# A written engine order, wide one-hot tables and another division of the q work in linear attention with a hash-routed MoE

## Chip, cores and metric

The kernel runs on one core of one Trainium2 chip. The metric is device time in microseconds of one execution, with every input in device memory (HBM) at the start and the output there at the end. Five engines work side by side, each through its own instructions in their order: TensorE (PE, matrix products; the loading of weights is shown apart as PEld), VectorE (DVE), ScalarE (ACT), GpSimd (POOL) and SyncE (SP). They wait for each other with semaphores. Transfers are started by SP (a hardware queue) or by POOL (a software queue, also for gathers and scatters of rows) and run on sixteen DMA engines.

## The reference

Linear attention over 8 batches and 8 heads, 576 tokens, 64 dimensions, is followed by a mixture of eight experts in which a hash of the token's id picks the expert.

```python
q_s = np.exp(q - np.max(q, axis=-1, keepdims=True))
q_s = q_s / (np.sum(q_s, axis=-1, keepdims=True) + 1e-09)
k_s = np.exp(k - np.max(k, axis=2, keepdims=True))
k_s = k_s / (np.sum(k_s, axis=2, keepdims=True) + 1e-09)
kv = np.einsum('bhsd,bhse->bhde', k_s, v)
x = np.einsum('bhsd,bhde->bhse', q_s, kv)
x = x.transpose(0, 2, 1, 3).reshape(4608, 512)

expert_idx = token_ids * np.int64(2654435761) % np.int64(8)
for e in range(8):
    mask = expert_idx == e
    h = np.maximum(x[mask] @ w1[e], 0.0)        # 512 -> 1024
    out[mask] = h @ w2[e]                       # 1024 -> 512
```

## The kernel before

**Slots.** Each expert has 640 slots: a cell of 72 for each of the 8 batches, and 64 overflow slots for tokens beyond a cell. 640 slots are five blocks of 128 rows. If some cell or overflow overfills, a general path (`_any_routing`) runs instead; it is not taken with these inputs.

**Index** (`_Index`). Tokens lie 36 to a partition on 128 partitions. VectorE takes the expert from the id (L82, L84), builds a one-hot table EH over 8 experts × 36 columns (L88), and from counts and prefix sums (the scan in L147 and `_pick`, L156 and L158) each token's rank and slot. `tables` then turns slots into row numbers: for each of the 36 columns VectorE compares a row of 0..127 with the slot's low seven bits (L252, one 128 × 128 table of zeros and ones for each column), and TensorE adds up 36 products of such a table with BV, the slot's block number times the token's own number (L256). The result is `gidx`, one row number for each slot. A second set of 36 tables (L278, L281) gives `oidx`, the rows of overflowing tokens.

**Keys** (`_Attention.keys`). For each batch SP loads k and v (1.18 MB each, through six raw buffers), ACT takes exp of k (L344), POOL (b < 4) or VectorE (b ≥ 4) casts v to f16 (L347), TensorE adds up 72 products (L354), and VectorE divides by the sums (L357 to L363) into `kvr`, one 128 × 128 block-diagonal matrix for each batch and pair of heads.

**Queries.** POOL gathers rows of q in the order of the slots, five blocks for one expert (L371). `soften` takes exp on ACT (L382) and divides by the sum on VectorE (L384 to L387). `turned` transposes a block on TensorE (four products, L396) and copies it out on VectorE (L398) to qT. `product` multiplies qT with kvr for three batches and two experts at once (L408), and ACT copies the result out (L410) to XT, the input of a pair of experts. `overflow` and `shared` (L418, L421, L431, L437, L439) do this for all overflow slots through tables Q (L684).

**Experts** (`_Moe.expert`). A group of eight products (L472, 128 × 320) gives two of the eight 128-wide slices of the hidden layer for one half of the slots; relu goes to ACT (L477) and VectorE (L479) in turn. After eight groups, five blocks of eight products (L484, 128 × 512) give the output, which VectorE (L488) and ACT (L490) take out in turn, and POOL scatters (L492). POOL also fetches weights, four halves of 0.5 MB for each expert (L453), one expert ahead, in two buffers.

**What sets the order.** The program is written in order of need, and a scheduler places instructions of each engine by its own estimate of readiness. Tiles carry the waits. Ten blocks (experts 0 and 1) and four overflow blocks are prepared ahead of the experts. From then on, while a pair of experts runs, the q work of the next pair waits in `queue`; after each of an expert's 13 steps `side` takes two items out:

```python
            def side():
                for _ in range(2):
                    if queue:
                        queue.pop(0)()
```

Of the kernel before, what the change touches and what calls it, by code (L numbers as in the profile page):

```python
# [40 lines left out]
class _Index:  # L41

    def __init__(self, nc, token_ids, cpool, ipool, ps):
        self.nc, self.ipool, self.ps = nc, ipool, ps
        self.count = 0  # L50
        V = nc.vector
        ids = ipool.tile([128, NCH, 2], I32)
        nc.sync.dma_start(ids[:].rearrange("q m w -> q (m w)"), token_ids.bitcast(I32))

        rowi = cpool.tile([128, CAP], F16)
        self.rowi = rowi
        nc.gpsimd.iota(rowi[:], [[1, CAP]], channel_multiplier=0, allow_small_or_imprecise_dtypes=True)
        pidf = cpool.tile([128, 1], F32)
        self.pidf = pidf
        nc.gpsimd.iota(pidf[:], [[0, 1]], channel_multiplier=1, allow_small_or_imprecise_dtypes=True)  # L60
        eio = ipool.tile([128, E_MOE, NCH], F16)
        nc.gpsimd.iota(eio[:], [[1, E_MOE], [0, NCH]], channel_multiplier=0, allow_small_or_imprecise_dtypes=True)
        bio = ipool.tile([128, NBP, C9], F32)
        self.bio = bio
        nc.gpsimd.iota(bio[:], [[2 * CELL, NBP], [0, C9]], channel_multiplier=0, allow_small_or_imprecise_dtypes=True)

        half = cpool.tile([128, 1], F32)
        V.tensor_scalar(out=half[:], in0=pidf[:], scalar1=63.5, scalar2=None, op0=ALU.is_gt)
        self.half = half

        hrow = ipool.tile([128, 128], F16)
        V.tensor_single_scalar(hrow[:], rowi[:, 0:128], 63.5, ALU.is_gt)
        own = ipool.tile([128, 128], F16)
        V.tensor_scalar(out=own[:], in0=hrow[:], scalar1=half[:, 0:1], scalar2=None, op0=ALU.is_equal)
        lower = ipool.tile([128, 128], F16)
        V.scalar_tensor_tensor(out=lower[:], in0=rowi[:, 0:128], scalar=pidf[:, 0:1], in1=own[:],
                               op0=ALU.is_gt, op1=ALU.mult)
        ones = ipool.tile([128, 128], F16)
        nc.gpsimd.memset(ones[:], 1.0)

        ei = ipool.tile([128, NCH], I32)
        V.tensor_single_scalar(ei[:], ids[:, :, 0], 7, ALU.bitwise_and)  # L82
        ef = ipool.tile([128, NCH], F16)
        V.tensor_copy(ef[:], ei[:])  # L84
        self.ef = ef
        EH = ipool.tile([128, E_MOE, NBP, C9], F16)
        EHf = EH[:].rearrange("p e n c -> p (e n c)")
        V.tensor_tensor(out=EH[:].rearrange("p e n c -> p e (n c)"), in0=eio[:],  # L88
                        in1=ef[:].unsqueeze(1).to_broadcast([128, E_MOE, NCH]), op=ALU.is_equal)
        EC = ipool.tile([128, E_MOE, NBP], F16)  # L90
        with nc.allow_low_precision("counts up to 9"):
            V.reduce_sum(EC[:], EH[:], axis=AX.X)

        pa = ps.tile([128, 2, 512], F32, tag="S")
        NE = E_MOE * NCH
        nc.tensor.matmul(pa[:, 0, 0:NE], lhsT=lower[:], rhs=EHf, start=True, stop=True)
        nc.tensor.matmul(pa[:, 1, 0:NE], lhsT=own[:], rhs=EHf, start=True, stop=True)
        pb = ps.tile([128, 2, 512], F32, tag="S")
        NEN = E_MOE * NBP
        for j in range(2):  # L100
            s = slice(64 * j, 64 * j + 64)
            nc.tensor.matmul(pb[:, j, 0:NEN], lhsT=ones[s, :], rhs=EC[s].rearrange("p e n -> p (e n)"),
                             start=True, stop=True)

        ov_be = ipool.tile([128, B_, E_MOE], F32)
        V.tensor_scalar(out=ov_be[:].rearrange("p (n j) e -> p j e n", j=2),
                        in0=pb[:, :, 0:NEN].rearrange("p j (e n) -> p j e n", n=NBP), scalar1=float(CELL),
                        scalar2=0.0, op0=ALU.subtract, op1=ALU.max)
        ov_eb = ipool.tile([128, E_MOE, B_], F32)
        V.tensor_copy(ov_eb[:], ov_be[:].rearrange("p b e -> p e b"))  # L110
        pb_ = ipool.tile([128, B_, E_MOE], F32)
        self._excl(pb_[:], ov_be[:], B_, E_MOE)
        pe_ = ipool.tile([128, E_MOE, B_], F32)
        self._excl(pe_[:], ov_eb[:], E_MOE, B_)
        self.ov_be, self.ov_eb = ov_be, ov_eb
        run = ipool.tile([128, E_MOE * NBP, C9], F32)
        tot = ipool.tile([128, E_MOE * NBP, C9], F32)
        V.tensor_copy(tot[:], pa[:, 1, 0:NE].rearrange("p (g c) -> p g c", c=C9))
        self._excl(run[:], tot[:], E_MOE * NBP, C9)
        V.tensor_tensor(out=run[:], in0=run[:], in1=pa[:, 0, 0:NE].rearrange("p (g c) -> p g c", c=C9), op=ALU.add)  # L120
        EH4 = EH[:]
        self.rank = self._pick(EH4, run[:].rearrange("p (e n) c -> p e n c", e=E_MOE))

        def mine(t):
            d = self._new(ipool, [128, E_MOE, NBP])
            V.tensor_tensor(out=d[:], in0=t[:, :, :, 1], in1=t[:, :, :, 0], op=ALU.subtract)
            V.scalar_tensor_tensor(out=d[:], in0=d[:], scalar=half[:, 0:1], in1=t[:, :, :, 0],
                                   op0=ALU.mult, op1=ALU.add)
            return d[:].unsqueeze(3).to_broadcast([128, E_MOE, NBP, C9])

        ob = self._pick(EH4, mine(pb_[:].rearrange("p (n j) e -> p e n j", j=2)))
        is_ov = ipool.tile([128, NCH], F32)
        self.is_ov = is_ov
        V.tensor_single_scalar(self.is_ov[:], self.rank[:], float(CELL) - 0.5, ALU.is_gt)
        self.ob = ob
        self.rb = self._pick(EH4, mine(pe_[:].rearrange("p e (n j) -> p e n j", j=2)))

    def _new(self, pool, shape):
        self.count += 1
        t = pool.tile(shape, F32, name=f"ix{self.count}")  # L140
        return t

    def _excl(self, out, x, g, n):

        V = self.nc.vector
        xf = x.rearrange("p g n -> p (g n)")
        V.tensor_tensor_scan(out=out.rearrange("p g n -> p (g n)"), data0=xf, data1=xf, initial=0.0, op0=ALU.add,  # L147
                             op1=ALU.bypass)
        V.tensor_tensor(out=out, in0=out, in1=x, op=ALU.subtract)
        b = self._new(self.ipool, [128, g])  # L150
        V.tensor_copy(b[:], out[:, :, 0])
        V.tensor_tensor(out=out, in0=out, in1=b[:].unsqueeze(2).to_broadcast([128, g, n]), op=ALU.subtract)
# [67 lines left out]
    def tables(self, gidx, oidx, tpool):  # L220
# [53 lines left out]
        for n in range(NBP):  # L274
# [5 lines left out]
            for c in range(C9):  # L280
# [14 lines left out]
                        op1=ALU.min)  # L295
        return ov


class _Raw:


# [495 lines left out]
```

The softmax here doesn't subtract the row's maximum and nothing guards it: scores larger than these inputs give would overflow.

## Time and profile before

| | us |
|---|---|
| median of 14 runs | 284.67 |
| range of these runs | 283.87 to 289.28 |
| the profiled execution's own time | 285.23 |
| its span, from the first to the last instruction | 283.4 |
| first product of an expert (L472) | 117.90 |
| the four pairs of experts end at | 161.56, 201.21, 240.56, 276.5 |

Busy shares over the span: PE 72%, PEld 45%, DVE 63%, ACT 33%, POOL 46%. The mean clock granted to TensorE was 0.836 of full speed.

Lines of a group read: source line, engine, operation, tile written <- tiles read, shapes, count | busy us in total, mean ns of one | idle time of the engine just ahead of them, and what ended it. A table by stretches reads: from:to in us, length, then busy us (and number of instructions) for PE, PEld, DVE, ACT and POOL, the granted clock, the DMA engines' share and GB/s. The line PEclk has one digit for each fortieth of the span: 9 is full speed, 5 is half.

### The profile page before, as it was taken

To read this page: it belongs to the slowest core of one execution; us is meant where nothing else is said; L and a number is where in the kernel's file an instruction comes from. 1 tells how busy PE (TensorE), PEld (TensorE's weight loads), DVE (VectorE), ACT (ScalarE), POOL (GpSimd) and SP (SyncE) were. 2 spreads that over 40 slices of the span, in tenths; PEclk is the share of its full clock that TensorE was granted. 3 is DMA by queue.
4 is the path that set the end of the run, shared out by engine and by line. 5 is a ranking of instruction groups with operands and counts; after the bars stand their busy time and mean duration, and the time that the engine had idled before them with its cause. 6 is when DMAs were issued, how large, how long until landed. Compare 5 with 4: busy or idle time off the path is not lost. (4 is left out here: it accounts for less than half of the span.)

```text
span 283.4 us, 4832 instructions
## 1 busy us (share of the span) xinstructions
PE 202.7 (72%) x1836; PEld 128.9 (45%) x1836; DVE 179.4 (63%) x484; ACT 94.2 (33%) x151; POOL 131.0 (46%) x148
## 2 busy tenths in 40 slices
PE   0070295711313386999969999999999999899990
PEld 0060164601201274574636575665674664655640
DVE  6999995808279994899799269983353231333310
ACT  2532001109215335442842144851222731211210
POOL 9873307435708874218782723614504415315033
PEclk9996555555555556899999999999999999999996
DMA  6999999982623445199988996895969759934022
GB/s 251 425 429 323 317 324 421 418 319 75 167 63 103 129 107 157 12 202 256 237 237 175 205 226 106 214 165 94 239 133 161 206 100 204 193 82 161 0 75 105
DMA packets 13804, 55.38 MB, mean 195 GB/s; under 512 B 2898, under 2 KB 2898, under 8 KB 11728
## 3 DMA queue, kind: packets, MB, share of 16 engines
q0 software_dynamic: 11328, 36.11, 54.5%
q1 hardware_dynamic: 2448, 18.91, 16.3%
q8 instruction: 16, 0.26, 0.4%
q14 instruction: 12, 0.10, 0.1%
HBM read 64.00 MB, written 10.49 MB: 263 GB/s over the span
## 5 line engine op out<-in xcount | busy, mean ns | idle before, releaser
L484 PE MATMUL po<-w2r,hT 128*128 128x512 f16 x320 | 73.3, 379 | 0.0
L371 POOL DMA_INDIRECT qraw<-in_q_dram,gidx x40 | 46.6, 1164 | 41.4 <-ACT q L382 22.4
L492 POOL DMA_INDIRECT out_dram<-ob,gidx x40 | 41.4, 1036 | 50.6 <-DVE ob L488 35.3
L472 PEld LDWEIGHTS <-w1r 128*128 128x128 f16 x512 | 48.8, 98 | 21.0 <-issue 2.7
L472 PE MATMUL ph<-XTn,w1r 128*128 128x320 f16 x384 | 56.9, 299 | 0.9 <-DVE hT L479 0.8
L484 PEld LDWEIGHTS <-hT 128*128 128x128 f16 x320 | 30.6, 98 | 32.7
L488 DVE TENSOR_SCALAR ob<-po 128x512 f32<-128x512 f32 x24 | 16.6, 691 | 44.8 <-PE po L484 22.7
L479 DVE TENSOR_SCALAR hT<-ph 128x640 f16<-128x640 f32 x32 | 26.3, 822 | 21.6 <-PE ph L472 20.0
L396 PE MATMUL pq<-ident,q 128*128 128x128 f16 (+1 forms) x176 | 18.8, 238 | 27.7 <-DVE q L387 15.8
L477 ACT ACTIVATE hT<-ph 128x640 f16<-128x640 f32 x32 | 22.5, 702 | 46.5 <-PE ph L472 44.4
L382 ACT ACTIVATE q<-qraw 128x512 f16<-128x512 f32 x44 | 24.4, 620 | 38.0 <-DMA qraw<-in_q_dram,oidx 13.7
L384 DVE TENSOR_REDUCE rq<-q 128x8 f32<-128x512 f16 x44 | 29.6, 678 | 8.2 <-ACT q L382 8.2
L387 DVE TENSOR_TENSOR q<-q,rq 128x512 f16<-128x512 f16 x44 | 30.0, 685 | 0.1
L344 ACT ACTIVATE k<-t 128x2304 f16<-128x2304 f32 x8 | 16.9, 2117 | 37.7 <-remote 20.3
L396 PEld LDWEIGHTS <-q 128*128 128x128 f16 (+1 forms) x176 | 12.7, 106 | 36.0 <-issue 17.5
L453 POOL DMA_DIRECT2D w1r<-in_moe_w_dram x16 | 9.2, 581 | 40.0 <-PE ph L472 19.5
L354 PE MATMUL pt<-t,k 64*64 64x65 f16 x576 | 20.4, 242 | 6.6 <-DVE rq L385 1.9
L490 ACT ACTIVATE ob<-po 128x512 f32<-128x512 f32 x16 | 9.5, 597 | 46.5 <-PE po L484 39.4
L354 PEld LDWEIGHTS <-k 64*64 64x64 f16 x576 | 17.8, 153 | 7.6 <-issue 5.3
L472 PE MATMUL ph<-XTp,w1r 128*128 128x320 f16 x128 | 19.7, 299 | 0.8 <-ACT hT L477 0.8
L408 PE MATMUL px<-qT,kvr 128*128 128x144 f16 x128 | 14.6, 240 | 5.2 <-issue 2.6
L410 ACT CAST XTn<-px 128x432 f16<-128x432 f32 (+1 forms) x36 | 15.8, 482 | 6.1 <-PE px L408 4.6
(128 smaller groups left out, 186.9 us busy)
## 6 DMA issues: line engine op xcount, KB each, us to landing
t<-in_k_dram SPq DMA_DIRECT2D x8, 1152.0 KB, 13.4
t<-in_v_dram SPq DMA_DIRECT2D x8, 1152.0 KB, 12.7
w1r<-in_moe_w_dram POOLq DMA_DIRECT2D x16, 512.0 KB
w2r<-in_moe_w_dram POOLq DMA_DIRECT2D x16, 512.0 KB
qraw<-in_q_dram,gidx POOLq DMA_INDIRECT x40
out_dram<-ob,gidx POOLq DMA_INDIRECT x40
qraw<-in_q_dram,oidx POOLq DMA_INDIRECT x4
ids<-in_moe_token_ids_dram SPq DMA_DIRECT2D x1, 36.0 KB, 1.9
```

The costliest lines, as they stand in the source:

```text
L344: nc.scalar.activation(k16[:].rearrange("p c d -> p (c d)"), kraw[:], ACT.Exp)
L354: nc.tensor.matmul(pkv[s, r, 0:DH_ + 1], lhsT=k16[s, r * C9 + c, :], rhs=v16[s, r * C9 + c, 0:DH_ + 1], start=(c == 0), stop=(c == C9 - 1))
L371: nc.gpsimd.indirect_dma_start(out=raw[:, i, :], out_offset=None, in_=self.q[:, :], in_offset=bass.IndirectOffsetOnAxis(ap=idx[:, c0 + i:c ...
L382: nc.scalar.activation(qv.rearrange("p h d -> p (h d)"), raw[:, i, :], ACT.Exp)
L384: nc.vector.reduce_sum(rq[:], qv, axis=AX.X)
L387: nc.vector.tensor_tensor(out=qv, in0=qv, in1=rq[:].unsqueeze(2).to_broadcast([128, H_, DH_]), op=ALU.mult)
L396: nc.tensor.transpose(pv[:, r, 0:w], q16[0:w, i, 2 * r:2 * r + 2, :].rearrange("p h d -> p (h d)"), self.ident[0:w, 0:w])
L472: nc.tensor.matmul(ph[:, i, :HN], lhsT=w1r[:, dc, fc * 128:(fc + 1) * 128], rhs=XTp[:, e % 2, dc, g * HN:(g + 1) * HN], start=(dc == 0), s ...
L477: nc.scalar.activation(hv, ph[:, :, :HN], ACT.Relu)
L479: nc.vector.tensor_relu(hv, ph[:, :, :HN])
L484: nc.tensor.matmul(po[:], lhsT=hT[:, fc, blk * 128:(blk + 1) * 128], rhs=w2r[:, fc, :], start=(fc == 0), stop=(fc == FC - 1))
L492: sc = nc.gpsimd.indirect_dma_start(out=self.out[:, :], out_offset=bass.IndirectOffsetOnAxis(ap=self.gidx[:, gb:gb + 1], axis=0), in_=ob[: ...
```

## The change

The order is written by hand for all five engines in the first phase, and for PE, ACT, DVE and SP in the second; there the scheduler places POOL alone.

- **Index.** ACT spreads 0..127 over 36 columns into `wide`; VectorE compares all of it with the slots' low bits in one instruction of 4,608 elements (`A`). TensorE takes column `ch` of it as weights, so that neighbours lie 36 elements (72 bytes) apart; BV has the same layout. Ranks come from one scan over EH and three small matrix products. A second index `qidx` serves the gathers of q, and `gidx` the stores.
- **POOL.** The memsets of two q buffers (128 × 2560 each) and of eight kvr tiles go; VectorE clears kvr in one instruction, POOL clears the overflow buffer in four. v is cast on ACT for b < 4.
- **Ahead of the experts:** the five blocks of expert 0 and four of overflow, with their copies out on ACT, and products of six batches for expert 0. Two of expert 0's steps take the rest of its products, the last overflow block and `shared`.
- **q work among the experts' steps:** expert 0 takes expert 1's and the beginning of 2's; expert 1 the rest of 2's, 3's and the products for 2 and 3 (48 items); expert 2 takes 4's; expert 3 takes 5's and products (34 items); 4 takes 6's; 5 takes 7's and products. There are three buffers for gathered q, not two.
- **Relu** is on ACT alone; the output is taken out by VectorE alone, except every second block of the last expert.
- **Weights.** w1 lies in two halves by hidden units. Expert 0's w1 waits for batch 6's exp of k, its w2 for batch 7's. Raw buffers: five, not six.

```diff
+        wide = tpool.tile([128, 128, NCH], F16, name="wide")
+        nc.scalar.copy(wide[:], rowi[:, 0:128].unsqueeze(2).to_broadcast([128, 128, NCH]))
...
-        for n in range(NBP):
-            A = tpool.tile([128, C9, 128], F16, tag="A")
-            for c in range(C9):
-                ch = n * C9 + c
-                V.tensor_scalar(out=A[:, c, :], in0=self.rowi[:, 0:128], scalar1=slo[:, ch:ch + 1], scalar2=None,
-                                op0=ALU.is_equal)
+        A = self.tpool.tile([128, 128, NCH], F16, tag="A")
+        V.tensor_tensor(out=A[:], in0=self.wide[:], in1=over(slo, 128), op=ALU.is_equal)
...
+        for ch in range(NCH):
+            self.nc.tensor.matmul(self.pg, lhsT=self.A[:, :, ch], rhs=self.BV[:, 0:2, :, ch],
+                                  start=(ch == 0), stop=(ch == NCH - 1))
...
-        for b in range(B_):
-            t = cpool.tile([128, NPAIR, 128], F16, name=f"kvr{b}")
-            nc.gpsimd.memset(t[:], 0.0)
+        nc.vector.memset(kvr[:], 0.0)
...
-        eng = nc.gpsimd if b < 4 else nc.vector
-        eng.tensor_copy(v16[:, :, 0:DH_], vraw[:].rearrange("p (c d) -> p c d", d=DH_))
+        if on_act:
+            self.nc.scalar.copy(dst, src)
+        else:
+            self.nc.vector.tensor_copy(dst, src)
...
-                if f2 % 2 == 0:
-                    nc.scalar.activation(hv, ph[:, :, :HN], ACT.Relu)
-                else:
-                    nc.vector.tensor_relu(hv, ph[:, :, :HN])
-                side()
+                nc.scalar.activation(hv, ph[:, :, :HN], ACT.Relu)
+                side(step)
+                step += 1
...
+        mctx.enter_context(tc.manual_schedule(engines={ENG.PE, ENG.Activation, ENG.DVE, ENG.Pool, ENG.SP}))
...
+        ix.slot_rows()
+        ix.slot_index(gidx, qidx)
+        at.gather(qraws[0], qidx, 0, BPE, MAINC - 128 * (BPE - 1))
...
+        at.gather(qrawo, oidx, 0, NBP)
+        at.gather(qraws[1], qidx, BPE, BPE, MAINC - 128 * (BPE - 1))
...
+        last[6] = exp_k(6)
+        gate(moe.fetch(wts, 0, 1)[0], last[6])
...
+        last[7] = exp_k(7)
+        gate(moe.fetch(wts, 0, 2)[0], last[7])
+        at.norm(6)
+        cast_v(7, False)
+        xovs[2] = at.overflow(2, qTo)
+        at.keys(7)
+        at.norm(7)
+        first = {
+            0: [lambda: [at.product(q0, X0, r, range(6, 8)) for r in range(NPAIR)],
+                lambda: xovs.update({3: at.overflow(3, qTo)})],
+            1: [lambda: at.shared(0, xovs, Qs), lambda: at.shared(1, xovs, Qs), lambda: overs(XTs[0], 0, 0)],
+        }
...
+        with tc.manual_schedule(engines={ENG.PE, ENG.Activation, ENG.DVE, ENG.SP}):
+            def stages(e):
+                bl = blocks(e, qraws[e % 3])
+                seq = []
+                for i in range(BPE + 2):
+                    if i < BPE:
+                        seq.append(bl[i][0])
+                    if 0 <= i - 1 < BPE:
+                        seq.append(bl[i - 1][1])
+                    if 0 <= i - 2 < BPE:
+                        seq += [bl[i - 2][2], bl[i - 2][3]]
+                return seq
...
+            plan = {1: lambda: rest.pop() + stages(3) + products([2, 3]),
+                    2: lambda: stages(4), 3: lambda: stages(5) + products([4, 5]),
+                    4: lambda: stages(6), 5: lambda: stages(7) + products([6, 7])}
...
+                    items = stages(1) + products([1]) + two[:6]
+                    rest.append(two[6:])
...
+                    upto = (len(items) * (step + 1 - skip) + 12 - skip) // (13 - skip)
+                    while done[0] < min(upto, len(items)):
+                        items[done[0]]()
+                        done[0] += 1
```

In the changed kernel the products of an expert are L442 and L452, relu L446, the copies out of the last layer L458, keys L318, the two table products L212 and L250, a block's exp L347, its division L352 to L355, its transposes L363, products L380, and `wide` L76.

## The prediction

> **What bounds the kernel now.** I read the clock and busy slices first, then the idle time ahead of each group, then stretches of the timeline. The kernel has two halves: until 117.90 us, the first L472 in the timeline, it prepares; then TensorE runs the experts until 276.52.
>
> ```profile
> PEclk9996555555555556899999999999999999999996
> DMA  6999999982623445199988996895969759934022
> ```
> A slice is 7.1 us. TensorE runs at half clock from 28 to 106 us, at full clock after about 115. DMA is full for the first 60 us, then hardly used until 117.
>
> ```profile
> 80.00:100.00 20.00, 6.62 (x74) 4.48 (x74) 19.75 (x57) 7.43 (x11) 12.04 (x9) 0.50 0.32 88
> 117.90:161.56 43.66, 40.39 (x281) 24.23 (x280) 36.50 (x96) 18.50 (x35) 26.17 (x29) 1.00 0.93 204
> 161.56:201.21 39.65, 39.52 (x281) 24.37 (x280) 27.17 (x66) 17.90 (x34) 15.03 (x19) 1.00 0.81 170
> 201.21:240.56 39.35, 39.25 (x282) 24.36 (x280) 14.17 (x24) 12.92 (x24) 14.59 (x19) 1.00 0.80 170
> 240.56:276.50 35.94, 35.12 (x209) 20.25 (x207) 10.65 (x14) 8.01 (x12) 10.30 (x12) 1.00 0.39 105
> ```
> Busy time of PE, PEld, DVE, ACT, POOL, then clock, DMA share and GB/s, for one stretch of preparation and for the four pairs of experts. VectorE bounds 80–100; from 117.9 TensorE does, with 154.28 busy of 158.60.
>
> What held preparation back shows in single groups and in the clock between 106 and 114:
>
> ```profile
> L82 DVE TENSOR_SCALAR ei<-ids 128x36 int32<-128x36 int32 x1 | 8.3, 8282 | 2.7 <-DMA ids<-in_moe_token_ids_dram 2.7
> L84 DVE CAST ef<-ei 128x36 f16<-128x36 int32 x1 | 2.0, 2017 | 0.0
> L252 DVE TENSOR_SCALAR A<-rowi,slo 128x128 f16<-128x128 f16 x36 | 7.3, 277 | 0.0
> L357 DVE TENSOR_SCALAR rec<-pt 128x4 f32<-128x4 f32 x8 | 1.3, 161 | 7.1 <-remote 7.0
> L278 DVE TENSOR_SCALAR A<-rowi,pos 128x128 f16<-128x128 f16 x36 | 7.4, 271 | 3.0 <-remote 2.8 <-PE po L281 0.2
> L88 DVE TENSOR_TENSOR EH<-eio,ef 128x288 f16<-128x288 f16 x1 | 0.3, 301 | 0.0
> L156 DVE TENSOR_TENSOR m<-EH,run 128x288 f32<-128x288 f16 x1 | 0.5, 452 | 0.0
> ```
> ```profile
> 108.00:110.00 2.00, 1.02 (x15) 0.72 (x14) 0.69 (x1) 1.16 (x3) 1.20 (x2) 0.58 0.68 193
> 112.00:114.00 2.00, 1.89 (x14) 1.17 (x14) 1.83 (x5) 0.85 (x3) 0.00 (x0) 0.50 0.12 49
> ```
> L82 and L84 process 36 elements in 10.3 us: POOL's memsets (L331, L335) run over the first, its cast (L347) over the second. The two "remote" waits have no work behind them that the trace names. The clock can fall back though TensorE is half busy.
>
> **The index.** The memsets and early casts leave POOL's head, so L82 and L84 should cost some .2 each: −9.9. The 36 instructions of L252, at a pitch of about .165 (5.9 us), become one comparison of 4,608 f16 elements. L88 and L156 give its two bounds: with the same 288 elements in .30 and .45 and some .15 fixed, .52 or 1.04 ns an element, so 2.55 or 4.95; both operands are f16 as in L88, so 2.55, −3.4. BV's three (1.66, 1.65, .59) become three at .9: −1.2. The row table is thus ready 14.5 earlier than gidx's 42.97, about 28.5. ACT's table copy is twice L344's width, some 4.1 us, before VectorE needs it.
>
> The 72 table matmuls now take weights 72 bytes apart. L256's pitch at half clock was .17 with contiguous weights; no row of before has strided ones. Bounds: no gain or loss, or a weight load at three times L256's 36 × .14 = 5.0 us, +10 on each table, 20 where both lie on the path. I take nothing, as L256 is nearest, and keep the 20.
>
> The Trainium skill, "SBUF — State Buffer", section "Door 1: The DMA port swizzle", speaks against this: it holds that SBUF reads pay at each new 16-byte line, so that only strides up to 8 bf16 elements are free. By it every one of these weights pays; it gives no price, so the sum by it lies toward the 20 that I kept as a bound.
>
> **Ahead of the first expert.** Ten blocks and four overflow blocks become five and four. A block held VectorE for about 1.79 between 80 and 100 (L384 .68, L385 .14, L386 .20, L387 .68, small gaps), so −9.0. Evictions L398 of nine blocks move to ACT: 9 × .42 = −3.8. After the last preparation, before spends 104.3 to 117.9 (13.6) on pair products, overflow and shared; after needs only 24 product matmuls and ACT's copies, about 3: −10.6. First expert matmul: 117.9 − 14.5 − 9.0 − 3.8 − 10.6 = 80.0. VectorE takes v casts only for b ≥ 4, as before (4 × 1.34); ACT takes the other four, 2.1 each, while loads are still landing. That cover would cost 8.5 if gone. This 80.0 keeps the unnamed waits of 7.0 and 2.8.
>
> POOL's queue now holds expert 1's weights and expert 3's five gathers ahead of expert 0's weights, since memory frees in that order. Each gather waits for a block's exponential of expert 0. POOL pays 5 × 1.3 for the gathers and about .6 for each weight half; expert 0's weights wait for k exponentials 6 and 7 anyway. I cost it at nothing, covered by the block stretch; without that cover, +5 to +8 from the landing of 2 MB at about 2.5 us a half MB alone and 5 when shared.
>
> **The experts.** Expert matmuls alone: 64 × .136 + 40 × .2155 = 17.35 an expert, 138.8. Moved behind the start or kept there: 35 blocks of transposes × .22 = 7.7; products 6 + 1.8 + .5; shared 16 × .2155 = 3.5; overflow .5; keys(7) 2.2. So 161.0 of work, 2.4 above 158.6, if nothing else binds.
>
> But the order binds. Relu is on ACT alone (32 × .82 leave VectorE), and q's blocks sit in the first slots of every expert that has any. ACT's in-order slot then holds relu .70, exp .62 and a copy .52; a block costs VectorE 1.81 + .42 = 2.27 with gaps, against 1.09 for a group of eight matmuls. The transposes stand in TensorE's queue, and all later expert matmuls behind them.
> - Experts 3 and 5: 34 items over 13 slots, all five blocks within the first eight. VectorE needs 5 × 2.27 = 11.35, and 2.1 before the first transpose; TensorE has 8.7 + 1.1. So 3.7 lost, plus about 1.5 on twelve product copies through two buffers: 17.35 + 1.1 + 2.0 + 5.2 = 25.7 each.
> - Expert 1: 48 items; nine blocks, 9 × 2.27 = 20.4, against 12.6 of TensorE work in the slots that hold them: 7.8 lost; 17.35 + 2.0 + 2.0 + 7.8 + 1.0 = 30.2.
> - Expert 0: 17.35, plus 6.7 of moved work, 1.1 and 1.8 for expert 1's blocks and products, 3.2 of waiting between its first two groups (keys(7), its kvr, the rest of the products, ACT's copies), and about 6 of the block chain: 36.2.
> - Experts 2 and 4 have five blocks over 13 slots: 18.9 each. Experts 6 and 7 have none: 17.35 each.
>
> Sum: 36.2 + 30.2 + 18.9 + 25.7 + 18.9 + 25.7 + 34.7 = 190.3. To this 158.60 − 154.28 = 4.3 of idle time as in before (weights and stores landing). For the clock: before stayed at half until 115 with TensorE 51 to 95% busy; expert 0's 36 us hold about 27 of work. Bounds: 0, if it is full from the first matmul; 8, if a stretch like 106–115 precedes. I take 4.
>
> The skill's "TensorE: Matmul & The Clock Gate", Part 1, has activity windows of about 3.4 us and a fall to half when idle. The trace agrees in part only, as 112–114 was at .50 with 95% busy. By the rule one window would cost under 2 us instead of 4.
>
> End of TensorE: 80.0 + 190.3 + 4.3 + 4 = 278.6. The last eviction, store and landing took 283.4 − 276.5 = 6.9; alternate evictions of the last expert stay split. Span 285.5. The profiled run took 285.23 around a span of 283.4, so +1.8: **287.3 us**, against 285.23 for that execution and 284.67 for the median. A difference under 0.5%, 1.4 us, can't be told from no change.
>
> **The rivals.** *The unnamed waits do not come back* (the other side). They sit at L357 and L278, both behind instructions whose order is rewritten. If both go, the start is 70.2 and the time 287.3 − 9.8 = 277.5. It decides alone as soon as more than 4.0 of the 9.8 is gone. For it: TensorE's matmuls for L357 were recorded at 73–74, its release at 79.66. Against: TensorE's program is as long as before, and the loads are the same.
>
> *The order does not bind.* Engines have slack where my slots are pessimistic; the experts then cost 161.0 + 4.3: 80 + 165.3 + 8.7 = 254, with the clock's 4, 258. For it: pairs two and three are 99.7% busy with the same blocks. Against: there, VectorE had two experts' time for ten blocks, and a scheduler placed them.
>
> *Strided weights are slow.* +5 to +20, thus 292 to 307; likely one table's 10, 297. For it: nothing in before reads so. Against: the gathers wait on loads until about 62 anyway, so part is hidden.
>
> *Expert 0's weights come late*, behind POOL's hoisted queue: +5 to +8, 292 to 295. *The change doesn't do what it says*: the built order does move the relus, the blocks and the index as described, so only the wide comparison at 1.04 ns an element is left, +2.4 a table, inside the forecast's range.
>
> **How the numbers follow.** Forecast .37, own range 281 to 294 (clock 0 to 8, a third of the order's 32 us lost or won back); of it .22 slower, .08 same, .07 faster. Unnamed waits gone .27: .25 faster, .02 same. Order not binding .08 faster. Strided .21 and late weights .07, both slower. Faster .40, same .10, slower .50. The range goes from 270, leaving out most of the .08 and a few hundredths of the waits' case, to 303, leaving out the worst strided end.
>
> **What would show it.** The row gather starts at about 29 us instead of 43.25; the first L442 stands at about 80; TensorE is idle 5 us in experts 3 and 5 and 8 in expert 1, released by VectorE's q or ACT's relu; experts 6 and 7 take 17.4. A pitch well over .2 for the table matmuls shows the strided rival; L442 released by a weights' DMA, the late one; no long "remote" wait, the first. An end of the experts under 165 us after their start makes the prediction wrong at its main step.

## The result and the profile after

The changed kernel takes 295.99 us (median of 10 runs, 293.06 to 296.94) against 284.78 for the kernel before in the same comparison: ratio 1.0414, 95% interval 1.0385 to 1.0443. It is slower, as forecast, but by 11.2 us where 2.6 were forecast; its profiled execution took 295.94.

| us, profiled executions | before | forecast | after |
|---|---|---|---|
| first product of an expert | 117.9 | 80.0 | 84.4 |
| from there to the last product | 158.6 | 198.6 | 197.3 |
| from there to the end of the span | 6.9 | 6.9 | 12.5 |
| around the span | 1.8 | 1.8 | 1.8 |
| sum | 285.2 | 287.3 | 296.0 |

The first phase is 33.5 shorter, the experts 38.7 longer, the end 5.6 longer. The forecast's shortfall of 8.7 is 4.4 at the start and 5.6 at the end, less 1.3 in the experts.

The clock and DMA slices of the changed kernel (7.4 us each):

```profile
PEclk9999999999787997999899999999999999999985
DMA  7999999996709457388936999285699195621130
```

The nines of the first phase are not to be taken at their word: the record of the clock starts only at 73.3 us here. Four transposes take .59 at 53.63 and .58 at 78.99, in a stretch recorded at .50, but .38 at 102.04, in one at 1.00. So TensorE ran nearly all of its preparation at half clock, as before. The experts begin at full clock and lose it in three spells of 3.4 us, from 90.4, 110.9 and 145.0.

The experts as a table by stretches (columns as before: PE, PEld, DVE, ACT, POOL busy, clock, DMA share, GB/s), one row for each of experts 0 to 5, and one for 6 and 7:

```profile
84.42:123.91 39.49, 30.56 (x284) 17.48 (x282) 20.67 (x46) 17.50 (x34) 18.00 (x19) 0.91 0.55 137
123.91:156.46 32.55, 25.11 (x176) 14.48 (x174) 21.55 (x51) 13.90 (x26) 16.61 (x18) 0.95 0.71 176
156.46:175.43 18.97, 18.72 (x127) 11.17 (x125) 13.40 (x31) 8.30 (x14) 12.67 (x14) 1.00 0.91 203
175.43:201.66 26.23, 21.30 (x158) 13.18 (x157) 13.65 (x31) 13.26 (x25) 7.61 (x10) 1.00 0.65 139
201.66:220.69 19.03, 18.72 (x126) 11.15 (x125) 13.51 (x31) 7.90 (x13) 6.80 (x9) 1.00 0.79 161
220.69:246.93 26.24, 21.32 (x158) 13.20 (x157) 13.64 (x31) 13.26 (x25) 7.72 (x10) 1.00 0.62 134
246.93:281.67 34.74, 34.74 (x209) 20.17 (x207) 5.80 (x10) 12.47 (x18) 10.75 (x12) 1.00 0.37 101
```

Experts 2 and 4 keep TensorE over 98% busy; 3 and 5 leave it idle for 4.9 each, 1 for 7.4, 0 for 8.9. No other engine is near full over a whole expert, nor is DMA in the idle ones, so this looks like waiting in order. One group of waits (engine, what waits <- what ended it: us in total, times, longest) makes up most of the 26.8 us:

```profile
PE pq L363 <- DVE q L355: 17.1, 15, 2.3
```

The transposes stand in TensorE's queue and wait for VectorE's division.

Groups by line and form, of the index and of the products of k and v:

```profile
L205 DVE TENSOR_TENSOR A<-wide,slo 128x4608 f16<-128x4608 f16 x1 | 2.6, 2552 | 0.0
L212 PE MATMUL pt<-BV,A 128*128 128x80 f16 x36 | 5.7, 336 | 8.0 <-DVE A L205 8.0
L335 POOL DMA_INDIRECT qraw<-in_q_dram,qidx x40 | 45.3, 1132 | 46.7 <-DVE qidx L222 24.0 <-ACT q L347 11.3 <-issue 6.7
L318 PE MATMUL pt<-t,k 64*64 64x65 f16 x576 | 20.2, 235 | 9.5 <-issue 6.1 <-ACT t L305 1.7 <-ACT k L300 1.1
L324 DVE TENSOR_SCALAR rec<-pt 128x4 f32<-128x4 f32 x8 | 1.3, 160 | 18.7 <-PE pt L318 12.1 <-remote 6.6
```

The comparison took 2.55, the lower of the two bounds. POOL's first gather follows at 28.57. But L318 has 6.1 us of "issue", time in which TensorE waited for nothing that the trace names, and VectorE's L324 behind it waited 18.7.

Stretches of the end, after the last product:

```profile
284.00:286.00 2.00, 0.00 (x0) 0.00 (x0) 0.00 (x0) 0.00 (x0) 0.00 (x0) 0.74 0.34 114
286.00:288.00 2.00, 0.00 (x0) 0.00 (x0) 0.00 (x0) 0.00 (x0) 0.00 (x0) 0.50 0.02 4
```

The last bytes of the stores move at 286.8, and the span goes on for 7.4 us more. The trace's records of instructions that the page doesn't count as busy tell why: GpSimd's DRAIN, ahead of the closing barrier, runs from 283.80 for 9.54 us. Before, it ran from 278.24 for 4.03, to .9 us after the stores' last byte.

### The profile page after: what moved, and what is told of

The parts are those of the page before. It is cut to its first block, busy times and chain, and to the rows that moved or that the text cites. A ratio compares the mean times of both kernels' runs of the same rounds, so it can differ in the third digit from the quotient of the medians.

```text
span 294.2 us, 4829 instructions
## 1 busy us (share of the span) xinstructions
PE 204.3 (69%) x1867; PEld 129.1 (44%) x1867; DVE 158.3 (54%) x374; ACT 125.5 (43%) x187; POOL 112.4 (38%) x134
## 3 DMA queue, kind: packets, MB, share of 16 engines
q1 hardware_dynamic: 2448, 18.91, 16.2%
## 4 chain that ended last, share of the span: by engine, by line
PE 50%; DVE 32%; ACT 6%; issue 5%; another core or an unknown queue 2%; POOL 0%; POOLq 0%; ACTq 0%; DVEq 0%
PE po L452 23%; PE ph L442 13%; DVE q L355 7%; DVE rq L352 6%; PE pt L318 5%; PE px L380 3%; DVE rq L354 2%; DVE rq L353 2%; ACT X L382 2%; PE pt L212 2%; DVE qT L370 2%; PE pq L363 2%; DVE t L307 1%; ACT q L347 1%
## 5 line engine op out<-in xcount | busy, mean ns | idle before, releaser
L452 PE MATMUL po<-w2r,hT 128*128 128x512 f16 x320 | 76.2, 388 | 0.0
L446 ACT ACTIVATE hT<-ph 128x640 f16<-128x640 f32 x64 | 45.0, 703 | 67.6 <-PE ph L442 64.0
L458 DVE TENSOR_SCALAR ob<-po 128x512 f32<-128x512 f32 x38 | 26.2, 690 | 76.0 <-PE po L452 72.4
L442 PE MATMUL ph<-X,w1r 128*128 128x320 f16 x448 | 65.3, 299 | 0.6 <-ACT hT L446 0.6
L335 POOL DMA_INDIRECT qraw<-in_q_dram,qidx x40 | 45.3, 1132 | 46.7 <-DVE qidx L222 24.0
L442 PEld LDWEIGHTS <-w1r 128*128 128x128 f16 x512 | 49.2, 98 | 20.8 <-issue 1.6
L363 PE MATMUL pq<-ident,q 128*128 128x128 f16 (+1 forms) x176 | 18.0, 229 | 38.7 <-DVE q L355 34.4
L452 PEld LDWEIGHTS <-hT 128*128 128x128 f16 x320 | 30.6, 99 | 32.5 <-issue 1.8
L363 PEld LDWEIGHTS <-q 128*128 128x128 f16 (+1 forms) x176 | 11.8, 102 | 48.5 <-issue 28.7
L352 DVE TENSOR_REDUCE rq<-q 128x8 f32<-128x512 f16 (+1 forms) x44 | 29.8, 677 | 5.8 <-ACT q L347 4.3
L382 ACT CAST X<-px 128x432 f16<-128x432 f32 (+1 forms) x44 | 18.9, 467 | 30.8 <-PE px L380 30.4
L355 DVE TENSOR_TENSOR q<-q,rq 128x512 f16<-128x512 f16 (+1 forms) x44 | 30.4, 692 | 1.5
L318 PE MATMUL pt<-t,k 64*64 64x65 f16 x576 | 20.2, 235 | 9.5 <-issue 6.1
L347 ACT ACTIVATE q<-qraw 128x512 f16<-128x512 f32 (+1 forms) x40 | 24.0, 625 | 0.0
L318 PEld LDWEIGHTS <-k 64*64 64x64 f16 x576 | 17.2, 146 | 12.9 <-issue 9.7
L380 PE MATMUL px<-qT,kvr 128*128 128x144 f16 (+1 forms) x160 | 15.2, 227 | 6.2 <-ACT X L382 4.2
L380 PEld LDWEIGHTS <-kvr 128*128 128x128 f16 x160 | 11.4, 105 | 12.8 <-issue 7.7
L370 DVE COPY qT<-pq 128x512 f16<-128x512 f16 (+1 forms) x35 | 13.5, 389 | 0.5
```

The lines of the kernel that those rows point to most:

```text
L318: self.nc.tensor.matmul(pkv[s, r, 0:DH_ + 1], lhsT=k16[s, r * C9 + c, :], rhs=v16[s, r * C9 + c, 0:DH_ + 1], start=(c == 0), stop=(c == C9 ...
L335: nc.gpsimd.indirect_dma_start(out=raw[0:w, i, :], out_offset=None, in_=self.q[:, :], in_offset=bass.IndirectOffsetOnAxis(ap=idx[0:w, c0 + ...
L347: nc.scalar.activation(q16[0:w].rearrange("p h d -> p (h d)"), raw[0:w, i, :], ACT.Exp)
L352: nc.vector.reduce_sum(rq[0:w], q16, axis=AX.X)
L355: nc.vector.tensor_tensor(out=q16, in0=q16, in1=rq[0:w].unsqueeze(2).to_broadcast([w, H_, DH_]), op=ALU.mult)
L363: nc.tensor.transpose(pv[:, r, 0:w], q16[0:w, 2 * r:2 * r + 2, :].rearrange("p h d -> p (h d)"), self.ident[0:w, 0:w])
```

## The experiments

The runs went to several chips, and the kernel before took 271 to 276 us on most of them and 285 to 287 on two; so each run is read beside the kernel before on its own chip, and stages are compared rather than times. The stages come from one profile each; the times are medians of four to six runs for the two rows of the changed kernel without and with whole gathers, for spread and for scheduled and spread with and without whole gathers, and single runs for the rest.

| run | first product | experts | end | time | before there |
|---|---|---|---|---|---|
| changed kernel, again | 73.7 | 198.1 | 12.5 | 285.90 | 273.38 |
| second phase scheduled | 73.6 | 168.4 | 12.5 | 256.44 | 272.46 |
| relu split | 73.5 | 211.8 | 12.5 | 299.52 | 272.46 |
| spread | 73.2 | 181.9 | 12.5 | 269.46 | 272.46 |
| POOL held back | 71.6 | 199.0 | 12.5 | 284.84 | 272.46 |
| both phases scheduled | 82.0 | 167.2 | 12.5 | 263.63 | 273.38 |
| scheduled, gathers of 128 | 73.6 | 168.8 | 6.6 | 250.72 | 273.38 |
| scheduled and spread | 73.5 | 167.0 | 12.5 | 255.09 | 273.38 |
| the same, gathers of 128 | 73.9 | 169.5 | 6.5 | 251.04 | 273.45 |
| changed kernel, gathers of 128 | 73.4 | 198.2 | 6.9 | 280.21 | 273.45 |
| spread, transposes later | 73.5 | 181.7 | 12.5 | 269.50 | 273.45 |
| scheduled, weights side by side | 76.7 | 170.3 | 12.5 | 261.37 | 273.45 |
| gathers of 128, heads ahead | 74.4 | 197.6 | 6.6 | 280.37 | 271.29 |
| gathers of 128, heads earlier | 82.2 | 193.4 | 6.7 | 284.09 | 287.08 |

**The changed kernel itself** beside the others.

> The changed kernel itself beside these. Theory (on this chip TensorE's program does not run dry in the first phase, nor in the kernel before, as the variants' first product at 71.6 to 73.6 shows): first product 73.5, experts 197, drain 9.54, time 284 to 286 against about 272 before, ratio 1.04 to 1.05. Rival (the variants themselves removed the empty time): first product at 84, time 295 to 297.

Ratio 1.0462 (1.0438 to 1.0486). The first product stands at 73.7, so the variants' early start was no property of theirs: the same program loses 10.7 us there on one chip and not on another. The profile of the changed kernel and of this run, TensorE alone, over the same stretch:

```profile
36.14 1.25 PE L318 MATMUL pt<-t,k 64*64 64x65 f16 x33
37.79 2.67 PE L318 MATMUL pt<-t,k 64*64 64x65 f16 x76 [0.40 <-issue]
40.84 0.32 PE L318 MATMUL pt<-t,k 64*64 64x65 f16 x4 [0.39 <-issue]
...
47.33 0.33 PE L318 MATMUL pt<-t,k 64*64 64x65 f16 x4 [0.49 <-issue]
```
```profile
36.12 3.84 PE L318 MATMUL pt<-t,k 64*64 64x65 f16 x131
41.65 0.59 PE L318 MATMUL pt<-t,k 64*64 64x65 f16 x13 [1.69 <-issue]
42.17 0.61 PE L363 MATMUL pq<-ident,q 128*128 128x128 f16 x4
```

In the first, TensorE gets some four products every .73 us for 7 us; in the second the same 144 products are done by 42.2. The run with four half gathers (below), on a chip where before takes 285, trickles again, from 40.80 to 47.4. TensorE's "issue" time in L318 is 4.4 to 6.8 us in this run, in the two others on chips where before takes 285 to 287 and in the profile of after, and at most 2.0 in the runs on the other chips.

**The order of the second phase.**

```diff
-        with tc.manual_schedule(engines={ENG.PE, ENG.Activation, ENG.DVE, ENG.SP}):
+        if True:
```

> Second phase placed by the scheduler on all engines, the items and their slots as written. Theory (the written order binds: transposes stand in TensorE's queue before VectorE has the block): the stalls in experts 1, 3 and 5 shrink, the experts last 172 to 182 us instead of 197, time 271 to 281. Rival (not the order but the work that was moved in, or late weights and gathers, bound the experts): experts still 190 to 200, time 290 to 299. The end after the last product, 12.5 us in the changed kernel and 6.9 in the one before: if it belongs to the written order it falls to 7, if to the first phase or the stores it stays at 10 to 13.

The experts fell to 168.4, beyond the theory, with the same instructions; the end stayed. Expert 3, which both kernels begin with 16 products ahead of the first transposes: the changed kernel run again, and this one (TensorE alone):

```profile
164.38 2.34 PE L442 MATMUL ph<-X,w1r 128*128 128x320 f16 x16
169.30 0.38 PE L363 MATMUL pq<-ident,q 128*128 128x128 f16 x4 [2.59 <-DVE q L355]
169.52 2.34 PE L442 MATMUL ph<-X,w1r 128*128 128x320 f16 x16
...
175.48 0.39 PE L363 MATMUL pq<-ident,q 128*128 128x128 f16 x4
177.32 0.27 PE L363 MATMUL pq<-ident,q 64*128 64x64 f16 x4 [1.45 <-DVE q L355]
```
```profile
146.50 2.34 PE L442 MATMUL ph<-X,w1r 128*128 128x320 f16 x16
148.67 0.39 PE L363 MATMUL pq<-ident,q 128*128 128x128 f16 x4
148.90 2.34 PE L442 MATMUL ph<-X,w1r 128*128 128x320 f16 x16
151.07 0.39 PE L363 MATMUL pq<-ident,q 128*128 128x128 f16 x4
```

TensorE's order is the same, but the block isn't ready in the first. ACT tells why, in the same two kernels:

```profile
155.77 0.62 ACT L347 ACTIVATE q<-qraw 64x512 f16<-64x512 f32 x1
165.72 0.70 ACT L446 ACTIVATE hT<-ph 128x640 f16<-128x640 f32 x1 [9.34 <-PE ph L442]
166.32 1.14 ACT L347 ACTIVATE q<-qraw 128x512 f16<-128x512 f32 x2
```
```profile
144.92 0.63 ACT L347 ACTIVATE q<-qraw 128x512 f16<-128x512 f32 x1 [1.32 <-DVE rq L354]
147.79 0.70 ACT L446 ACTIVATE hT<-ph 128x640 f16<-128x640 f32 x1 [2.24 <-PE ph L442]
```

In the written order ACT stands idle for 9.34 us, because the next exp is queued behind the expert's first relu. The scheduler runs it 1.6 us before that expert starts. Of the 29.6 us between the two runs' experts, 24.9 − 3.6 = 21.3 are idle time of TensorE (198.07 − 173.20 and 168.45 − 164.89); the other 8.3 are busy time, in stretches whose clock was .87 and .95 where it is .94 and 1.00 when scheduled. By expert, 7.9 and 9.4 lie in experts 0 and 1, 5.3 and 6.1 in 3 and 5, and under 1 in all others. The lines above explain how expert 3 begins; experts 0 and 1, the larger part, were not taken apart.

**Relu as before.**

```diff
-                nc.scalar.activation(hv, ph[:, :, :HN], ACT.Relu)
+                if f2 % 2 == 0:
+                    nc.scalar.activation(hv, ph[:, :, :HN], ACT.Relu)
+                else:
+                    nc.vector.tensor_relu(hv, ph[:, :, :HN])
```

> Relu again on ACT and VectorE in turn, nothing else changed. Theory (VectorE's 2.27 us a block is the pace in the slots that hold blocks): 4 x .82 more on VectorE in every expert, so expert 1 +3, experts 3 and 5 +2 each, time 299 to 304. Rival (ACT's in-order slot of relu, exp and copy is the pace): 4 x .70 less on ACT, experts 1, 3 and 5 each 2 to 3 us shorter, time 286 to 291.

The experts take 13.7 more, twice the theory's 7 but on its side. So moving relu to ACT helped within the written order; the rival fell.

**Spread**, with the second phase still written.

```diff
-            plan = {1: lambda: rest.pop() + stages(3) + products([2, 3]),
-                    2: lambda: stages(4), 3: lambda: stages(5) + products([4, 5]),
-                    4: lambda: stages(6), 5: lambda: stages(7) + products([6, 7])}
+            plan = {1: lambda: rest.pop() + merge(stages(3), products([2])),
+                    2: lambda: merge(stages(4), products([3])), 3: lambda: merge(stages(5), products([4])),
+                    4: lambda: merge(stages(6), products([5])), 5: lambda: merge(stages(7), products([6])),
+                    6: lambda: products([7])}
```

`merge` interleaves two lists evenly.

> Each expert from 1 on takes the blocks of the expert two ahead and, merged between them over all 13 slots, the products of the next expert alone (8 groups of 4 products of 72 columns). Theory (order and pace of VectorE): experts 2 to 5 take 17.35 + 1.1 + 1.8 + about .5 = 20.8 each instead of 18.9, 26.3, 19.0, 26.2; expert 1 24 instead of 32.7; expert 6 19.2; experts together 39.5 + 24 + 83.2 + 19.2 + 17.35 = 183, time 280 to 283. Rival (work or transfers bound the experts): the added products cost 4 us and nothing is won, time 296 to 300.

Experts 0 to 7 took 40.0, 24.9, 20.1, 20.3, 20.4, 20.3, 18.4 and 17.5: 181.9 against the theory's 183; ratio to before .9897 (.9850 to .9944), a difference of under 2%. More even filling wins 16.2 us over the changed kernel's experts.

**Transposes one place later** in that order (`range(BPE + 3)` and `i - 3` for the last two items).

> The spread run with its written order, but a block's transposes and copy out stand one more place behind its division (three places behind its exp, not two). Theory (TensorE waits because the transposes stand too early in its queue): experts 2 to 5 from 20.3 to 19.7 each, experts 0 and 1 shorter by 1 to 3, time 262 to 267 against 269.5. Rival (VectorE's pace, not the place of the transposes): 268 to 271.

Experts 2 to 5 stay at 20.2 to 20.3, and what expert 0 won (2.0), expert 1 lost (1.9). Expert 0's gain is not less waiting: TensorE is idle for 7.8 us of it in both runs, but runs 6.8 us at half clock instead of 10.2. So a later place in TensorE's queue mends nothing; that ACT and VectorE are what is late is then the reading left. Two more runs moved that, in the changed kernel with gathers of 128 rows.

**Heads ahead**: the first two exps and the first division of the next blocks go to the end of the expert before, for experts 2 to 5.

```diff
+            def head(x):
+                held[x] = stages(x)
+                return held[x][:3]
-                    2: lambda: stages(4), 3: lambda: stages(5) + products([4, 5]),
+                    2: lambda: held[4][3:] + head(5), 3: lambda: held[5][3:] + products([4, 5]) + head(6),
```

> The changed kernel with whole gathers and its written order, but the first two exps and the first division of the blocks that experts 2 to 5 take stand at the end of the expert before, ahead of that next expert's first relu. Theory (in the written order ACT stands idle for some 9 us before an expert's first relu, and the exp behind it makes the first transpose late; the scheduler's gain lies in starting these earlier): experts 3 and 5 from 26.2 to 22.5 to 24, experts 2 and 4 from 19.0 to 18.6, TensorE's longest wait before a transpose there under 1.5 us. Rival (VectorE's pace over all five blocks sets the length, wherever they begin): 25.5 to 26.5 and 19.0. On a chip where before takes 273: 274 to 276 by the theory, 279 to 281 by the rival.

Experts 3 and 5 took 27.7 and 26.9, each with a spell of 3.4 us at half clock that costs some 1.3 of it (TensorE is busy for 22.6 and 22.7 instead of 21.3). Even without it this is a miss, and VectorE shows it.

```profile
165.66 0.69 DVE L458 TENSOR_SCALAR ob<-po 128x512 f32<-128x512 f32 x1 [3.03 <-DMA out_dram<-ob,gidx]
166.26 0.68 DVE L352 TENSOR_REDUCE rq<-q 128x8 f32<-128x512 f16 x1
```

The exps ran early, but the division stood behind the fifth copy out of the expert before, and that waited 3.03 for a store to free one of four output buffers.

**Heads earlier**: the same three items some four steps before the end.

> As the run with the heads ahead, but those two exps and the division stand some four steps earlier, ahead of the last copies out of the expert before. In the run with the heads at the very end, VectorE's division stood behind the fifth copy out, which waited 2.4 to 3.0 us for a store to free its buffer. Theory (the block chain starts late because of what stands ahead of it in ACT's and VectorE's queues): experts 3 and 5 from 26.2 to 22.5 to 24.5, TensorE's wait before the first transpose there under 1 us; time 273 to 277 where before takes 271 to 273. Rival (VectorE's pace over all five blocks): 25.5 to 27.5, time 279 to 281.

The first transposes now wait for nothing in both experts (172.86 and 217.73, directly behind eight products). Expert 5 takes 24.2, as the theory had it. Expert 3 stays at 25.9: VectorE's copy out waits 3.18 for a store again, now with the second division behind it, and the second transposes are late by 1.67. The later ones wait .3 to .7 each, VectorE's pace against one group and a transpose. So the order costs in two ways, a late start of the chain and then VectorE's pace, and the store's wait feeds the first. This is a part only: scheduled, experts 3 and 5 take 21.3 and 20.9, and all experts together take 193.4 with the heads earlier and 168.4 scheduled.

**Scheduled and spread.**

> Second phase placed by the scheduler, and the plan of the spread run (blocks two experts ahead, products one ahead). Theory (with the order free, what is left are VectorE's 24 us of blocks in expert 1 and the pairs' uneven load): experts 1 to 5 at 20 to 21 each, experts together 163 to 167 instead of 168.4, time 251 to 255. Rival (the scheduler has already levelled the load, and the 4 us of added products are paid in full): 257 to 262.

The experts take 167.0, the ratio is .9340 (.9318 to .9363). Experts 2 to 5 take 19.6 each, 78.4 instead of 79.3 without the spread, and expert 6 1.0 more for its added products: the scheduler had levelled most of the load already.

**Both phases scheduled** (the first phase's line goes too).

> No written order in either phase: the new index, blocks and plan, all placed by the scheduler. Theory (the first phase's gain is the shorter index, fewer blocks ahead and the moved copies, not the written order): first product of an expert within 5 us of the 73.6 of the run with only the second phase scheduled, time 254 to 262. Rival (the written order of the first phase earns its gain): first product at 85 to 100, time 268 to 283.

The first product moves from 73.6 to 82.0: the rival's direction, below its range. The written order of the first phase earns 8.4 us, and the trace shows where: TensorE is done at 69.0 with what stands ahead of the experts and then waits 13.1 us for w1r, of which POOL issues a half only at 76.35 (65.38 with only the second phase scheduled, on the same chip). So it earns this by when the weights are fetched, not by the order of the preparation's own work. The rest of that phase's gain then belongs to the index, the blocks and the copies, which were not taken apart.

**POOL held back**: expert 1's weights and the gathers for 2 and 3 wait, in the manner of the `gate` lines, for batch 7's exp of k.

> Expert 1's four weight halves and the gathers for experts 2 and 3 wait for batch 7's exp of k, so POOL's queue holds only the first 14 gathers and expert 0's weights before. Theory (TensorE's empty time in the products of k and v from 40 to 48 and 58 to 62, some 11 us, comes from these transfers crowding its instructions out): that time falls under 4, the first product of an expert stands at 74 to 78 instead of 84.4, time 285 to 290. Rival (it belongs to the place in TensorE's program, or to the loads of k and v): it stays at 9 to 13, first product 83 to 87, and expert 1 waits for its weights or q: time 296 to 302.

TensorE's "issue" time in L318 was .9, but on this chip it was small for every run. It wins 1.1 us against the changed kernel on another chip: the first product is 2.1 earlier, expert 1 is 2.6 longer. On the cause of the trickle it says nothing; that is open.

**The end.**

```diff
-            w = last if i == n - 1 else 128
+            w = 128
```

> As the run with the second phase scheduled, but the fifth gather of an expert fetches 128 rows as before, not 64. The drain that GpSimd does at the end took 9.54 us in the changed kernel and all four variants of it, 4.03 in the kernel before. Theory (the half gathers cause it): 4.0 us, the time 5.5 lower, 251. Rival (it comes from something else of the change): 9.54 again, time 256 to 258.

> The changed kernel with gathers of 128 rows and nothing else. Theory (the end's extra 5.6 us come from the half gathers alone): 285.9 - 5.9 = 280.0, drain 3.4 to 4.1, end of the last product within 0.7 us. Rival (the drain's length belongs to a phase placed by the scheduler): drain 9.54, 285 to 287.

The drain takes 3.45 and 3.73, and the end 6.6 and 6.9. In the changed kernel this alone takes the time from 285.90 to 280.21 (ratios to before 1.0462 and 1.0232, the latter 1.0152 to 1.0312). The gathers for each expert's fifth block fetch 64 rows in the changed kernel. How many such gathers does it take?

> The run with only the second phase scheduled, with the half gather (64 rows) for expert 0 alone; the other seven fetch 128 rows. Theory (each half gather leaves the drain its share): 3.45 + (9.54 - 3.45) / 8 = 4.2 us, time 251 to 252. Rival (one half gather is enough, whenever it runs): 9.54, time 256 to 257. Rival (only what runs late matters): 3.4 to 3.7, time 250 to 251.

> The same with the half gather for expert 7 alone. Theory (a share for each): 4.2 us, time 251 to 252. Rival (one is enough, whenever): 9.54, time 256 to 257. Rival (only what runs late matters): 9.54 here and 3.4 to 3.7 where expert 0 has it.

> The run with only the second phase scheduled, with half gathers for experts 0 to 3. One alone left the drain at 3.5 to 3.7, eight make it 9.54. Theory (a fixed 9.54 once a certain number of half gathers is reached, four or fewer): 9.54, time 256 to 258. Rival (reached only beyond four): 3.4 to 3.8, 250 to 252. Rival (it grows with their number): about 6, 253 to 255.

> The same with half gathers for experts 1 to 7, whole ones for expert 0. Theory (fixed 9.54 from some number up to seven): 9.54. Rival (all eight are needed, so that it is the end state of all eight that counts and not their number): 3.4 to 3.8. Rival (growing): 8 to 9.

From the instruction records, us:

```
half gathers of 8     drain    after the stores' last byte
0 (five runs)         3.4 to 3.7   .9
1 (expert 0, or 7)    3.54, 3.73   .9
4                     3.15        1.0
7                     9.54        7.3
8 (ten runs)          9.54        6.5 to 7.7
```

The times are 252.34 and 253.39 with one (before: 275.97) and 265.84 and 268.18 with four and seven (before: 285.26). It is a jump between four and seven, to a drain of 9.54 us to within 10 ns whatever the stores do, not a share for each. The four are those of experts 0 to 3 and the seven those of 1 to 7, so whether it is the number or the later ones together isn't separated; expert 7's alone doesn't do it. What GpSimd waits for in it no view shows.

**Weights side by side**: the tables' layout is turned round, [column, 128] for [128, column], with VectorE's second operand repeated along the innermost dimension.

> The run with only the second phase scheduled, but the two tables laid out with each column's 128 weights side by side; the comparison then has one operand repeated along the innermost dimension. Theory (weights 72 bytes apart cost little): 36 products 4.4 to 5.4 us instead of 5.7, the comparisons about 4.9 instead of 2.55, rows later by 1 to 2.5, time 256 to 260 against 256.4. Rival (the distance is what the products pay for): 36 products in 2.5 to 3.2 us, time 253 to 256.

The comparisons took 4.95 each (the forecast's upper bound to the digit), rows came 2.4 later, and the 36 products of the first table still took 5.7, a pitch of .153. So the weights' distance doesn't set it. BV, the moving operand with 80 columns, still lies 72 bytes apart; whether that does, no run shows. In the second table, with 3 columns, the pitch falls from .060 to .027, so there distant weights cost 36 × .033 = 1.2 us. 261.37 is 5 above the run it is derived from, more than the theory's 4: the first product is 3.1 later and the experts 1.9 longer. The run also holds one more copy on ACT, of 1.39 us.

**A version that beats both.** Second phase scheduled, spread, gathers of 128 rows:

> Second phase placed by the scheduler, blocks two experts ahead and products one ahead, gathers of 128 rows. Theory (the three effects add): 255.1 - 5.9 = 249.2, ratio to the kernel before .910 to .918. Rival (whole gathers crowd the weights, or the drain was hidden by other waits here): 251 to 256.

251.04 us against 273.45, ratio .9183 (.9133 to .9233). The time is just inside the rival's range, but not by its mechanism: expert 0 took 33.3 instead of 31.2, with 6.8 us at half clock where the run before had none. Without the spread the single run took 250.72; the two can't be told apart.

## Why the prediction was right and wrong

**The index: right, in part by luck.** qidx was ready at 28.3 (forecast 28.5) and the first gather began at 28.57 instead of 43.25. The three terms hold: L82 and L84 became .12 and .18, the comparison 2.55, BV's three .9 each. But two things that the sum left out cancelled: VectorE reached the id at 7.70 instead of 2.70, after its constants and the clearing of kvr, and the way from EH to BV took 8.5 instead of 13.45.

**The start: 4.4 too early.** "This 80.0 keeps the unnamed waits of 7.0 and 2.8" was borne out in size: on the chip of the profile the start is 10.7 later than on the other, against 9.8 kept, with waits in other places (L318, and L324 with a "remote" wait of 6.6 again). That these are the same waits isn't shown; in the kernel before, a trickle of four products stands at 72.38, just ahead of the wait of 7.0. Without them the sum gives 70.2 and the run measured 73.7. The 3.5 lie in "24 product matmuls and ACT's copies, about 3": in that run, from the last transposes (67.08) to the first expert product (73.71) it is 6.6, as two overflow blocks, the products of k and v for batch 6 and a wait of 1.0 for w1r stand between them.

**The experts: right as a sum, by its main terms.** Expert 1: 30.2 forecast, 32.55 measured; 3 and 5: 25.7 and 26.2; 2 and 4: 18.9 and 19.0; 6 and 7: 17.35 and 17.4; 0: 36.2 and 39.5. The 8.3 for idle time and clock covered expert 0 and 1. Some of this is luck: of the 198.6 forecast TensorE was to be idle for 33.6 (29.3 in the experts' terms and 4.3 as before) and at work for 165.0; measured are 26.8 and 170.5. That it is the order is shown by the scheduled run, where the same instructions take 168.4. The two mechanisms that the working named, relu ahead of exp in ACT's slot and VectorE's pace a block, were both seen, at work in experts 3 and 5; a third, VectorE's copy out waiting for a store, was not in it.

**The clock: right in size, in another place.** The 4 us stood for a stretch at half clock where the experts begin. TensorE begins them at full clock and loses it later in experts 0 and 1 (.91 and .95). It is busy for 9.6 of the three spells' 10.2 us, so some 4.8 us are lost; this is an estimate, half of the busy time at half clock. The prediction takes 112–114 at .50 with 95% busy as a sign against windows of some 3.4 us. But the recorded spells of both profiles last 3.41 us or multiples of it (but for the last, which ends with the trace), and before's from 108.33 to 115.16 is two of them, the first only partly busy; so that row doesn't speak against them.

**The end: the step that failed.** "The last eviction, store and landing took 283.4 − 276.5 = 6.9" was carried over as if nothing of the change reached it. It measured 12.5, and the cause is in the diff: the gathers of 64 rows, which the working left uncosted. Restoring 128 rows gives 6.9 again. This is the largest part of the miss: without these 5.6 us the time would have been 290.4, inside the forecast's own range of 281 to 294.

**The rivals.** *The unnamed waits do not come back*: by the times, such waits depend on the chip in both kernels (before is 9 to 14 us shorter there too, though no trace shows the kernel before there), so the ratio hardly changes, 1.041 and 1.046; as a path to a faster kernel it is refuted. *The order does not bind*: refuted, by 29.6 us. *Strided weights*: true in kind, 1.2 us in the second table and none in the first; far from the 20 kept as a bound. For the strided moving operand of the first table a bound is 36 × (.153 − .027) = 4.5 us, an estimate that takes the second table's pitch as the least; no run tests it. The .17 of L256, the nearest row in the prediction, doesn't either, as VectorE's tables came every .165 there. The Trainium skill's "SBUF — State Buffer", section "Door 1: The DMA port swizzle", agrees in direction: it has strides beyond a line of 16 bytes pay, and in the second table they do, .060 against .027 us for a weight load and its product; in the first, the weights' distance shows nothing. *Expert 0's weights late*: at most 1.0 us, by TensorE's wait for w1r in the repeated run; with both phases scheduled it is 13.1. *The change doesn't do what it says*: it does.

## What to carry to other kernels

A written order is worth what it knows: here it earns 8 us in one phase, by when the weights are fetched, and loses 30 in the other, so test them one phase at a time. Where work for the next stage shares in-order queues with relus and copies out, its first steps on ACT and VectorE belong ahead of the next stage's first relu and ahead of copies that may wait for a store. Here this took expert 5 from 26.2 to 24.2, and a later place of TensorE's part won nothing; the scheduler's order was better than both. And look at what stands after the last useful instruction: a small saving in gathers (64 rows instead of 128) cost 5.6 us at the closing drain.

## What the runs showed of the hardware

GpSimd's closing drain is 3.2 to 4.0 us with up to four gathers of 64 rows in the program and 9.54 with seven or eight. On some chips, among them the one of the first profiles, TensorE gets about four 64 × 65 products every .73 us for 7 us in the loading phase, where the same products are done 5 us earlier on others; with a second such stretch (58.27 to 61) and the waits behind both, the first expert product stands 10.7 us later. An operand repeated along its innermost dimension costs VectorE 4.95 instead of 2.55 us for 4,608 f16 elements. And the digits of PEclk show 9 before the clock's first record, whatever the clock: instruction durations (.59 or .38 us for four transposes) tell it there.
